# Another order of the steps in the steady batches of a three-stage mixer kernel

## The chip, the cores and the metric

The kernel runs on one core of a Trainium2 chip. The metric is the time of one execution on the device in microseconds (us), the median of several runs. The chip's engines work in parallel, each through its own list of instructions in order: TensorE (PE, with its weight loads shown as PEld), VectorE (DVE), ScalarE (ACT), GpSimd (POOL) and SyncE (SP), which here only issues DMAs. Where an instruction needs the result of another engine, or a buffer that another engine still reads, it waits on a semaphore, and all that stands behind it on its engine waits too.

## The reference

Three blocks follow each other for 8 batches of 576 rows. What matters here is the first two:

```python
q_s = softmax(q, axis=-1)            # each head's row of 64, with +1e-9 in the divisor
k_s = softmax(k, axis=2)             # over the sequence
kv = np.einsum('bhsd,bhse->bhde', k_s, v)
x = np.einsum('bhsd,bhde->bhse', q_s, kv)     # then heads side by side: 576 x 512

h = np.maximum(x @ w_in, 0.0)        # 576 x 1024
u, v = h[..., :512], h[..., 512:]
v_n = (v - mean(v)) / np.sqrt(var(v) + 1e-06)
v_s = np.einsum('ts,bsd->btd', w_spatial, v_n) + b_spatial[None, :, None]
y = (u * v_s) @ w_out
```

The third block takes y: theta = y @ w_theta, y·cos(theta) and y·sin(theta) mixed over the sequence with two 576 x 576 matrices, and a last product with w_ch. Its weights come as float64.

## The kernel before, in words

Every float32 product is made of three products of parts: each operand is split into a high part (rounded to the format that TensorE multiplies at full rate) and a low part (the rest), and hi·hi, hi·lo and lo·hi are summed in PSUM. So behind nearly every product stand a cast on ScalarE, which makes the high part, and a subtraction on VectorE or POOL, which makes the low part.

The kernel has two phases. In the first, a loop over the 8 batches runs the first two blocks and stores y; in the second, from about 600 us on, it runs the third block. The weights of the third block are converted from float64 (their bits are taken apart by integer steps on VectorE and ScalarE) during the first phase, a piece at a time, and stored to DRAM.

The order of the work in the first phase is written out by hand, as strings of words. `run` takes a string and emits, for each word, that step's instructions on all engines; there is no scheduler behind it. Batches 0 and 1 have strings of their own (`PLANS`), batch 7 too (`LAST`); batches 2 to 6 use `PLAN`. A number behind a word is the tile, or for words of q and k how many batches ahead; a `v` or `p` behind it puts the subtraction on VectorE or POOL. The words that matter:

- `V0`..`V4`: products of x with the v half of w_in for 128 rows (V4 for the last 64). `v`: ReLU on ScalarE (L488; for tile 4 L491 to L493), statistics on VectorE (L495 to L498), the power -1/2 on POOL (L499). `N`: normalisation on VectorE (L511), cast on ScalarE (L516; L519 and L520 for tile 4), subtraction on POOL (L517) or VectorE (L521).
- `U0`..`U3`: products with the u half; `r`: their ReLU on ScalarE (L535).
- `T0`..`T3`: transposes of the next batch's q on TensorE (L435, L438); `t`: their split (ScalarE L448, then L449). `X`: the product of that q with k·v, `x` its split. `S`: the spatial product of the normalised v; `G`: times u (VectorE L550), cast (ScalarE L551), subtraction (L552). `Y`: the last product, `y`: its copy (ScalarE L566) and store.
- q: `ldq` loads it, `qmax`, `qsub` (POOL L408), `qexp` (ScalarE L411), `qsum` (VectorE L422), `qmul` (POOL L430). k: `ldk`, `kmax` (VectorE L279 to L287), `kt`, `kr`, `kbc`, `kmb`, `ksub` (POOL), `kexp`; `K` the product of k and v (L353), `kn` its division (VectorE L368 to L385).
- `B`: the first half of a conversion (L219 to L244), after which the next pieces are loaded; `P`: its second half (L246 to L264), with two stores.

PSUM holds three buffers of two banks for V, K, U, T, X, S and Y (`big()`), so a product can only start when the buffer that was freed first has been read by whoever splits or rectifies it, and two buffers of one bank for the transposes of k's maximum. V0 of a batch needs the x of that batch, which the batch before made.

Of the kernel before, what the change touches and what calls it, by code (L numbers as in the profile page):

```python
# [30 lines left out]
ORDER = "u1 u0 u2 v3 u3 v2 v1 v0 s0 s3 s5 s2 s4 s1 o0 o2 o1 o3"  # L31
LOADS = "ldk1 ldq1 ldv1 ldw2 ldw4"
PLAN = (
# [3 lines left out]
)  # L37
PLANS = {
# [934 lines left out]
```

## Time and profile before

| | |
|---|---|
| median of 3 runs | 1045.49 us (1042.97 to 1045.59) |
| the profiled execution | 1045.59 us, of which the span of the trace is 1043.8 us |
| PE busy | 990.2 us, 95% of the span |
| PEld busy | 936.0 us, 90% |
| DVE, ACT, POOL busy | 636.5 us (61%), 417.3 us (40%), 385.6 us (37%) |
| V0 of batches 2, 3, 4 starts at | about 199, 265.8, 333.9 us |

A busy share is the part of the span in which an engine worked on an instruction. TensorE's is high, so the few microseconds in which it waits, and the engine that it then waits for, are what the order of the other engines' work can change. "Granted clock" is the share of TensorE's full clock (2.4 GHz) that it was given. In the rows of a timeline the first number is the start in us from the span's start, the second the duration in us, and brackets give the idle time of the engine just before and the engine, tile and line that ended it.

### The profile page before, as it was taken

How to read it: one execution, taken by the hardware profiler on the slowest of the kernel's cores; microseconds unless marked ns; L12 is line 12 of the kernel's file. 1: busy time of each engine (PE TensorE's matmuls, PEld its weight loads, DVE VectorE, ACT ScalarE, POOL GpSimd, SP SyncE). 2: the span in 40 equal slices, each digit the busy share in tenths (PEclk: the TensorE clock that was granted, in tenths of full speed). 3: DMA queues.
4: the chain of work that ended last, by engine and by line, in shares of the span. 5: the costliest groups of instructions: out<-in, count | busy, mean ns of one | idle time of the engine just before them, and what ended most of it. 6: DMA issues, size and time to landing. Idle time of an engine off the chain costs nothing.

```text
span 1043.8 us, 16301 instructions
## 1 busy us (share of the span) xinstructions
PE 990.2 (95%) x6688; PEld 936.0 (90%) x6688; DVE 636.5 (61%) x985; ACT 417.3 (40%) x671; POOL 385.6 (37%) x349
## 2 busy tenths in 40 slices
PE   4687999999999999999999999999999999999998
PEld 3567899999889899899999999999999999989998
DVE  7787868776676666766524745457363927374622
ACT  3545546543454444534524533234231515152410
POOL 6266147454545525545313323222132313121220
PEclk9888999999999999999999999999999999999999
DMA  7541441342414323431042336111111002010011
GB/s 262 192 126 41 175 163 43 133 158 85 178 68 159 120 92 113 158 110 44 21 167 81 126 125 136 46 46 47 56 46 47 37 10 90 13 57 35 2 46 46
DMA packets 37370, 96.50 MB, mean 92 GB/s; under 512 B 7088, under 2 KB 15792, under 8 KB 33200
## 3 DMA queue, kind: packets, MB, share of 16 engines
q1 hardware_dynamic: 33744, 85.96, 22.8%
q0 software_dynamic: 3552, 9.50, 3.2%
q8 instruction: 52, 0.85, 0.3%
q14 instruction: 22, 0.18, 0.1%
HBM read 67.08 MB, written 28.38 MB: 91 GB/s over the span
## 4 chain that ended last, share of the span: by engine, by line
PE 65%; DVE 10%; ACT 3%; issue 2%; DMA 1%; SPq 0%; ACTq 0%
PE ps L164 47%; PE pb L172 10%; PE ps L172 5%; DVE t L511 1%; PE pb L657 1%; DVE sm L495 1%; DMA st<-in_w_tok 1%; DVE q_s L422 1%; DVE t L282 1%; ACT u L535 1%; DVE kvl L385 1%; ACT vn L516 1%; DVE t L287 1%; PE ps L353 0%; DVE qt L449 0%
## 5 line engine op out<-in xcount | busy, mean ns | idle before, releaser
L164 PE MATMUL ps<-sp,vn 128*128 128x288 f32 x1472 | 211.7, 300 | 7.3 <-ACT vn L516 2.7
L164 PEld LDWEIGHTS ps<-sp,vn 128*128 128x128 f32 x1472 | 202.8, 192 | 9.9 <-ACT vn L516 2.9
L164 PE MATMUL ps<-g,wo 128*128 128x288 f32 x1104 | 160.6, 297 | 0.8 <-DVE wo L261 0.3
L164 PEld LDWEIGHTS ps<-g,wo 128*128 128x128 f32 x1104 | 151.0, 189 | 2.0 <-ACT t L566 0.7
L730 POOL TENSOR_TENSOR qt<-u,uh 128x576 fp32r<-128x576 f32 x31 | 44.2, 1426 | 217.7 <-ACT uh L728 217.7
L728 ACT CAST uh<-u 128x576 fp32r<-128x576 f32 x32 | 21.6, 674 | 216.1 <-DVE u L725 216.1
L164 PE MATMUL ps<-xh,w 128*128 128x288 f32 x512 | 93.4, 302 | 8.1 <-ACT w L257 8.1
L172 PE MATMUL ps<-w,xh 128*128 128x512 f32 x320 | 97.9, 398 | 3.3 <-ACT t L488 2.8
L164 PE MATMUL ps<-uh,w 128*128 128x288 f32 x496 | 91.8, 299 | 0.0
L164 PEld LDWEIGHTS ps<-xh,w 128*128 128x128 f32 x512 | 78.6, 194 | 9.1 <-ACT w L257 8.3
L172 PE MATMUL pb<-w,xh 128*128 128x512 f32 x256 | 81.3, 398 | 0.0
L552 POOL TENSOR_TENSOR g<-t,g 128x576 fp32r<-128x576 f32 x24 | 35.3, 1471 | 111.7 <-ACT g L551 111.7
L172 PEld LDWEIGHTS ps<-w,xh 128*128 128x128 f32 x320 | 59.2, 189 | 17.0 <-ACT t L488 3.5
L164 PEld LDWEIGHTS ps<-uh,w 128*128 128x128 f32 x496 | 73.6, 188 | 0.3
L499 POOL TENSOR_TENSOR mv<-mv,neg_half 128x1 f32<-128x1 f32 (+1 forms) x40 | 28.2, 709 | 91.7 <-DVE mv L498 91.6
L495 DVE BATCH_NORM_STATS2 sm<-t 128x6 f32<-128x512 f32 (+1 forms) x40 | 27.3, 682 | 52.3 <-ACT t L488 46.7
L725 DVE TENSOR_TENSOR u<-ps,kb 128x576 f32<-128x576 f32 x16 | 12.1, 758 | 73.6 <-PE ps L164 73.6
L164 PE MATMUL ps<-xl,w 128*128 128x288 f32 x256 | 56.0, 301 | 0.0
L172 PEld LDWEIGHTS pb<-w,xh 128*128 128x128 f32 x256 | 47.0, 188 | 9.8
L551 ACT CAST g<-t 128x576 fp32r<-128x576 f32 x32 | 21.6, 674 | 84.9 <-DVE t L550 84.8
L164 PE MATMUL ps<-sp,wo 128*128 128x288 f32 x336 | 53.9, 296 | 0.0
L164 PE MATMUL ps<-qt,w 128*128 128x288 f32 x248 | 53.0, 295 | 0.0
(208 smaller groups left out, 2029.2 us busy)
## 6 DMA issues: line engine op xcount, KB each, us to landing
vb<-in_v SPq DMA_DIRECT2D x8, 1300.0 KB, 6.3
y<-t SPq DMA_DIRECT2D x32, 288.0 KB, 2.3
out<-t SPq DMA_DIRECT2D x31, 288.0 KB, 2.1
qb<-in_q SPq DMA_DIRECT2D x7, 1152.0 KB, 5.2
kb<-in_k SPq DMA_DIRECT2D x6, 1152.0 KB, 7.8
st<-in_w_tok SPq DMA_DIRECT2D x9, 576.0 KB, 4.8
tok_d<-st SPq DMA_DIRECT2D x18, 288.0 KB, 2.2
qb<-y SPq DMA_DIRECT2D x4, 1152.0 KB, 5.2
```

Of the source, the lines that this page charges most:

```text
L164: nc.tensor.matmul(out=ps[:, c, 0:CH], lhsT=a, rhs=w[:, c * CH:(c + 1) * CH], start=first and i == 0, stop=final and i == last,)
L172: nc.tensor.matmul(out=ps, lhsT=a, rhs=w, start=(i == 0), stop=(i == last))
L282: nc.vector.tensor_tensor(out=m[p0:p0 + 64, c0:c0 + 256], in0=m[p0:p0 + 64, c0:c0 + 256], in1=kb[p0:p0 + 64, 2048:2304], op=ALU.max,)
L287: nc.vector.tensor_tensor(out=m, in0=m, in1=kb[:, c:c + 512], op=ALU.max)
L385: nc.vector.tensor_tensor(out=kl[p0:p0 + 64, :, :, e0:e0 + 64], in0=kn[p0:p0 + 64], in1=f(kh[p0:p0 + 64, :, :, e0:e0 + 64]), op=ALU.subtract,)
L495: nc.vector.bn_stats(out=bs[0:n], in_=vr[0:n])
L499: nc.gpsimd.tensor_tensor(out=mv[0:n, 1:2], in0=mv[0:n, 1:2], in1=neg_half[0:n, 0:1], op=ALU.pow)
L551: nc.scalar.copy(out=g_s[m], in_=g)
L552: eng.tensor_tensor(out=g_s[4 + m], in0=g, in1=f(g_s[m]), op=ALU.subtract)
L725: nc.vector.tensor_tensor(out=halves(u_s[m]), in0=ps[:, :, 0:CH], in1=halves(y1[b % 2][:, m, :]), op=ALU.add)
L728: nc.scalar.copy(out=st["uh"][:, m, :], in_=u_s[m])
L730: eng.tensor_tensor(out=qt_s[m], in0=u_s[m], in1=f(st["uh"][:, m, :]), op=ALU.subtract)
```

## The change

`PLAN`, the table of the steady batches, stands in another order; nothing else is touched. The first line of it before and after:

```diff
@@ -31,10 +31,10 @@
 PLAN = (
-    "qexp1 V0 V1 v0 v1 qsum1 V2 v2 qmul1 K1 ldv2 kn1 N0 V3 v3 ldk2 V4 v4 U0 N1 N2 U1 r0 B0p U2 N3 "
...
+        "V0 v0 N0 V1 qexp1 qsum1 qmul1 v1 V2 v2 K1 kn1 V3 V4 v3 v4 U2 N3 N4v N1 U0 ldk2 r0 N2 B0p ldv2 "
...
```

The words are the same, with these exceptions: one `B` has become `B0s` (that conversion's sign is taken on ScalarE and multiplied on, instead of set by a step on VectorE), and `G1` has become `G1v` (its subtraction on VectorE instead of POOL). What moves: v0's steps and N0 stand ahead of q's exponential, N3 and N4 ahead of N1 and N2, the u products come in the order 2 0 3 1, k's maximum stands ahead of S1 and G1, X1 behind S2, X2 behind Y0, the load of q behind S3, q's maximum and subtraction behind x product 2 and k's subtraction, and the last two conversions' second halves at the end.

On ScalarE at the start of a steady batch (q's exponential is L411, the ReLUs of v tiles L488, the cast of v tile 0 `vn_80`), before:

```order
L411 ACTIVATE qb<-qb 128x2304
L488 ACTIVATE t_3201<-ps 128x512
L488 ACTIVATE t_3209<-ps 128x512
L488 ACTIVATE t_3233<-ps 128x512
L384 CAST kvh<-kn 64x4x64 x2
L516 CAST vn_80<-t_3201 128x512
```

and after:

```order
L488 ACTIVATE t_3187<-ps 128x512
L516 CAST vn_80<-t_3187 128x512
L411 ACTIVATE qb<-qb 128x2304
L488 ACTIVATE t_3220<-ps 128x512
L488 ACTIVATE t_3241<-ps 128x512
L384 CAST kvh<-kn 64x4x64 x2
```

The ReLU and the cast of tile 0 moved ahead of the exponential, the other two ReLUs stayed behind it.

On ScalarE beside the u products (L535 are their ReLUs, `vn_81` to `vn_83` the casts of v tiles 1 to 3, `vn_88` and `vn_89` those of tile 4, L223 to L236 the first conversion's steps), before:

```order
L516 CAST vn_81<-t_2538 128x512
L516 CAST vn_82<-t_2562 128x512
L535 ACTIVATE u<-ps 128x576
L223 ACTIVATE t_2710<-t_2710,rebase 128x576
L235 ACTIVATE t_2712<-st 128x576
L236 ACTIVATE t_2711<-t_2711 128x576
L516 CAST vn_83<-t_2624 128x512
L519 CAST vn_88<-t_2642 64x512
L520 CAST vn_89<-t_2642 64x512
L535 ACTIVATE u<-ps 128x576
```

and after:

```order
L516 CAST vn_83<-t_2632 128x512
L519 CAST vn_88<-t_2640 64x512
L520 CAST vn_89<-t_2640 64x512
L516 CAST vn_81<-t_2549 128x512
L535 ACTIVATE u<-ps 128x576
L516 CAST vn_82<-t_2570 128x512
L223 ACTIVATE t_2716<-t_2716,rebase 128x576
L235 ACTIVATE t_2718<-st 128x576
L236 ACTIVATE t_2717<-t_2717 128x576
L535 ACTIVATE u<-ps 128x576
```

The casts of tiles 3 and 4 moved from between the first two ReLUs to ahead of the first, the cast of tile 2 to behind it; the conversion's three steps stay between the two ReLUs.

On VectorE beside the spatial products (`t_2891` and `t_2858` hold k's maximum, L550 are the gates' products with u, `qt_94` the low half of t2), before:

```order
L550 TENSOR_TENSOR t_2887<-ps,u 128x576
L279 TENSOR_TENSOR t_2891<-kb 128x512
L282 TENSOR_TENSOR t_2891<-t_2891,kb 64x256 x2
L287 TENSOR_TENSOR t_2891<-t_2891,kb 128x512 x2
L449 TENSOR_TENSOR qt_94<-ps,qt_93 128x576
```

and after:

```order
L279 TENSOR_TENSOR t_2858<-kb 128x512
L282 TENSOR_TENSOR t_2858<-t_2858,kb 64x256 x2
L287 TENSOR_TENSOR t_2858<-t_2858,kb 128x512 x2
L550 TENSOR_TENSOR t_2893<-ps,u 128x576
L552 TENSOR_TENSOR g<-t_2893,g 128x576
L449 TENSOR_TENSOR qt_94<-ps,qt_93 128x576
```

The product of gate 1 moved from ahead of k's maximum to behind it, and its subtraction, on POOL before, stands here too.

## Rows read from the trace of the kernel before

**Rows 1.** Waits of the weight loads, 190 to 542 us: us in total, times, longest

```profile
PEld ps L435 <- POOL vn L517: 7.3, 5, 1.8
PEld ps L164 <- DVE qt L449: 4.0, 7, 0.8
PEld ps L164 <- ACT u L535: 2.7, 5, 0.6
```

**Rows 2.** Timeline of TensorE in batch 3: V0, U0, last of U3, T0, S0, X0, X2

```profile
265.77 0.63 PE L172 MATMUL ps<-w,xh 128*128 128x512 f32 x2
...
283.65 0.43 PE L164 MATMUL ps<-xh,w 128*128 128x288 f32 x2
...
296.18 0.43 PE L164 MATMUL ps<-xh,w 128*128 128x288 f32 x2
298.17 0.63 PE L435 MATMUL ps<-turned,qb 128*128 128x128 f32 x4 [1.56 <-POOL vn L517]
...
299.23 3.99 PE L164 MATMUL ps<-sp,vn 128*128 128x288 f32 x28 [0.32 <-ACT u L535]
...
303.88 0.80 PE L164 MATMUL ps<-qt,kvh 128*128 128x288 f32 x4
...
314.28 0.79 PE L164 MATMUL ps<-qt,kvh 128*128 128x288 f32 x4 [0.56 <-DVE qt L449]
```

**Rows 3.** Timelines of ScalarE, VectorE and POOL in batch 3, V0 to T0

```profile
271.73 2.13 ACT L411 ACTIVATE qb<-qb 128x2304 f32<-128x2304 f32 x1 [4.09 <-POOL qb L408]
...
286.00 0.58 ACT L491 COPY t<-ps 64x512 f32<-64x512 f32 x1
...
291.79 0.77 ACT L223 ACTIVATE t<-t,rebase 128x576 int32<-128x576 int32 x1
...
297.43 0.64 ACT L535 ACTIVATE u<-ps 128x576 f32<-128x576 f32 x1
...
274.38 0.69 DVE L495 BATCH_NORM_STATS2 sm<-t 128x6 f32<-128x512 f32 x1 [6.16 <-ACT t L488]
...
280.45 0.32 DVE L368 TENSOR_SCALAR sm<-ps 64x4 f32<-64x4 f32 x2
...
281.92 1.71 DVE L385 TENSOR_TENSOR kvl<-kn,kvh 64x256 fp32r<-64x256 f32 x2
...
289.51 0.99 DVE L511 TENSOR_SCALAR t<-t,mv 128x512 f32<-128x512 f32 x2
...
292.59 1.67 DVE L241 SCALAR_TENSOR_TENSOR t<-st,t 128x576 int32<-128x576 int32 x1 [1.35 <-ACT t L223]
294.18 2.10 DVE L511 TENSOR_SCALAR t<-t,mv 128x512 f32<-128x512 f32 x2
297.56 0.82 DVE L521 TENSOR_TENSOR vn<-t,vn 64x512 fp32r<-64x512 f32 x1 [1.27 <-ACT vn L520]
...
293.82 1.73 POOL L237 TENSOR_TENSOR t<-t,t 128x576 f32<-128x576 f32 x1 [0.18 <-ACT t L236]
```

**Rows 4.** Batch 4: T0 and S0 (timeline); a stretch's busy times, then PEclk, DMA share, GB/s

```profile
366.31 0.63 PE L435 MATMUL ps<-turned,qb 128*128 128x128 f32 x4 [1.56 <-POOL vn L517]
...
367.37 5.48 PE L164 MATMUL ps<-sp,vn 128*128 128x288 f32 x28 [0.32 <-ACT u L535]
...
368.00:370.00 2.00, 2.00 (x10) 2.00 (x10) 1.97 (x4) 1.35 (x2) 0.00 (x0) 0.50 0.85 278
```

**Rows 5.** By line: ns min/median/max, first and last start; then batch 3's timeline

```profile
L511 DVE TENSOR_SCALAR t<-t,mv x39: 529/539/1653, 77.1 to 558.1; 128x512 f32<-128x512 f32 x31, 64x512 f32<-64x512 f32 x8
L282 DVE TENSOR_TENSOR t<-t,kb x16: 416/420/1568, 5.2 to 447.7; 64x256 f32<-64x256 f32 x16
...
310.11 2.00 DVE L282 TENSOR_TENSOR t<-t,kb 64x256 f32<-64x256 f32 x2
310.26 1.57 POOL L552 TENSOR_TENSOR g<-t,g 128x576 fp32r<-128x576 f32 x1 [3.55 <-ACT g L551]
```

**Rows 6.** DMA issues, 312 to 326 us: line, queue, count, KB each, us to landing

```profile
qb<-in_q SPq DMA_DIRECT2D x1, 1152.0 KB, 5.0
```

More of the change, by code (lines that the diff above doesn't have):

```diff
@@ L33 @@
 PLAN = (
[3 rows of a table removed]
-)
[3 rows of a table added]
+    )
 PLANS = {
```

4 rows, old and new, of the table PLAN are left out of this document.

## The prediction

> **What bounds the kernel now.** I read the busy shares first: TensorE is the busy engine almost everywhere, so what the change can give is the time in which TensorE waits inside the five batches that use the changed table (batches 2 to 6, from about 199 to 537 us of the span), and what it can cost is a new wait there. Next I read TensorE's waits in that stretch, on the weight loads, since the busy time of the matmuls includes a modelled tail that hides the small gaps [rows 1]. Three releasers stand there: 7.3 us before the first product of q's transposes (T0, once in each of the five batches), 2.7 us before the first spatial product (S0, once in each), 4.0 us before products of x that wait for a low half of q (X0 and X2). Together 14.0 us, 2.8 a batch. Then I read one batch, the one whose V0 starts at 265.77, to see the places [rows 2]: the last u product's last pair starts at 296.18 and T0 only at 298.17, S0 at 299.23 after another wait, X0 at 303.88, X2 at 314.28 after 0.56 idle.
>
> Why T0 is late is in the rows of the other engines [rows 3]. T0 writes into the PSUM buffer of the second u product, and that is freed by r1, the ReLU at 297.43 on ScalarE, which ended when T0 began. (The view of rows 1 names POOL's subtraction, which ended just before r1.) S0 needs the buffer of the third product, freed by the next ReLU. r1 was ready long before, but ScalarE works in order: ahead of it stand the casts of v tiles 3 and 4, and these wait for VectorE's normalisation at 294.18, which stands behind the conversion's step on VectorE (L241), which waits for ScalarE's first conversion step at 291.79. All of that is late because v0's ReLU stands behind q's exponential, which starts only at 271.73, 6.0 us after V0, when POOL has finished subtracting q's maximum.
>
> **The change part by part**, in times after a batch's V0 (for the batch of rows 2, U0 is at +17.9 and one u product lasts 3.2 us, so T0 could run at +30.7 and S0 at +31.1).
>
> *q's subtraction earlier, v0 and its normalisation ahead of q's exponential.* q's maximum now stands behind x product 2 instead of behind the last conversion, so POOL goes from k's subtraction straight to q's. I put POOL's end at about +2, where it was at +5.9 (q's exponential waited 4.09 us for it [rows 3]). ScalarE then does v0's ReLU at +3.1, VectorE its statistics (0.69 for L495, about 0.4 for the two small ones) and the normalisation (0.54 alone [rows 5]), ScalarE the cast by about +6.6, then q's exponential (2.13) to +8.7. Before, that exponential ended at +8.1. VectorE from there to kn (the division of k·v) took 6.6 us before (273.86 to 280.45 [rows 3]) with three v statistics in it; now two stand there, so about 5.5, and kn begins at +14.2 at the latest instead of at +14.7. v0's statistics and normalisation cost nothing: VectorE is idle there.
>
> *N3 and N4 ahead of N1, N2 and ahead of the conversion.* kn's 3.2 us (280.45 to the end of L385 at 283.63 [rows 3]) end at +17.3, v3's statistics at +18.3. v3's ReLU no longer waits for v0's cast. V4 ends at +17.9; its copy, addition, ReLU and statistics took 3.6 us before (286.00 to the normalisation at 289.51 [rows 3]) with 0.5 of queueing, so N3's normalisation starts at about +21.2. N3, POOL's power, N4, three casts and the subtraction L521: 4.2 us before (294.18 to 298.38), of which 1.1 is the slow pair of normalisations (2.10 against 0.99 for the pair at 289.51 [rows 3]); alone, with the power between, 3.6. So N1 starts at about +24.8. N1, its cast and r0 take 1.7: r0 ends at +26.5, and U1, which needs that buffer, starts at +27.5 (1.0 spare). N2's cast, the three ScalarE steps of the conversion (0.77 for the first [rows 3], about 2.0 for the three) and r2 end at +29.5: T0 at +30.7 has 1.1 spare. The next cast and r3 end at +30.7: S0 at +31.1 has 0.4 spare. Both waits go. What is late next is X0: POOL's addition for the conversion (1.73 at 293.82 [rows 3]) ends at +30.6, VectorE's six conversion steps and ScalarE's two follow, and t0's low half is ready at +35.4, with T1 finished at +35.4. I leave 0.1 to 0.2 a batch for X0 and 0.2 once for S0 in batch 2, whose exponential starts later, 1.2 us in all.
>
> *U products 2 0 3 1.* The same 96 matmuls. It only changes which ReLU frees whose buffer, as used above; zero.
>
> *k's maximum earlier, G1's low half on VectorE.* k's maximum now stands ahead of G1 on VectorE instead of behind it. Before, its second line (L282) ran beside POOL's subtraction for G1 and took 2.00 for the two where one alone takes 0.42 [rows 5]; X2 waited for what stood behind it. Now G1 has no POOL part, and G0's POOL part ends about 0.7 us before k's maximum starts. So k's maximum lasts 1.15 us less, G1's product ends about 7.3 us after X0's start, G1's low half and t2's low half about 9.5 after, and T3, which needs the latter's buffer, has its turn 10.0 after. X2 moves behind Y0, where its operands are long ready. So the 0.7 us of X2 go as well. If the two lines take 2.00 again, T3 waits 0.65 and S3 0.25: about the loss that X2 had before. I take the free value, since the only POOL step near it ends before, and keep the other for the range.
>
> *The q load behind S3, q's maximum behind X2.* The load of q takes 5.0 us [rows 6]; it is issued when T3 has read the old q, at about +46, so it lands at +51, and VectorE reaches q's maximum at about +52. Hidden. The loads of k and v change places, both are issued at +13 when k·v is done and needed some 25 and 60 us later: zero.
>
> *Conversions later.* Two of three now end in the Y products' shadow; VectorE has some 2 us left before v0's statistics. y1's copy last on ScalarE: its buffer is taken by V2, 5.6 us into the next batch, and the copy ends at +1.5. Zero.
>
> **The sum.** 14.0 us of waits go, 1.2 stay: 12.8. A second term: in the profiled execution S0 of batch 4 took 5.48 us instead of 3.99, because the granted clock fell to 0.50 (1.2 of 2.4 GHz) from 368 to 370 us, just after T0's wait of 1.56 us [rows 4]. Two other batches had the same wait and no fall, so the fall is not certain, but its cause among these rows is the pause, and the pause goes: 1.5 us. 1045.59 for the profiled execution (equal to the median of the runs, 1045.49) − 12.8 − 1.5 = 1031.3; I say 1031.5.
>
> **The rivals.** *1. VectorE and POOL collide in the new places.* N4's normalisation and POOL's subtraction for N3 become ready within 0.3 us of each other. The pair at 294.18 shows the price, 1.1 us [rows 3]; L511 reaches 1.65 us at worst [rows 5]. With 1.1 more, r3 ends 0.7 after S0 could start and X0 loses 0.5: 1.0 us more a batch, 5 in all, 1036.5. If k's maximum collides instead, 0.9 in four batches, 1035. For it: every v tile passes this place. Against: the power releases VectorE first.
> The Trainium skill (SBUF — State Buffer, section "SBUF: two separate sides") says the ports that VectorE and GpSimd share are an exclusive lock, held for the whole instruction by whichever starts first. By that rule, N4 would lose nothing if first and 1.3 us, a whole POOL subtraction, if second; the sum would be 1031.5 or about 1037. The trace agrees with an all-or-nothing price: L282's pair ended 0.28 us after POOL's subtraction [rows 5].
> *2. The chain only slides.* r2 now stands behind three conversion steps and two casts. If my chain is off by 2 to 3 us (a stage or temporary buffer not free in time), T0 and S0 wait as before: 1038 to 1047.
> *3. Slower: q's load becomes late.* On VectorE q's maximum stands ahead of the low half of x2, and Y2 needs the buffer which that frees. With the load landing at +51, Y2 at about +58 has 2.5 us spare. From a load of 7.5 us on, each further microsecond stops TensorE in four batches; to eat 14 us it must take 11 us, and at 12 it gives 1050. Against it: 5.0 us in the row, and no other large transfer near that place.
>
> **How the numbers follow.** Forecast, 1029.5 to 1034: 0.60. Rival 1, 1034 to 1037.5: 0.22. Rival 2: 0.08 faster than 1042, 0.05 within 0.3%. Rival 3 or another new wait, slower: 0.05. So faster by over 0.3% (3.1 us, about what a measurement of this kernel can tell from no change) 0.90, within 0.05, slower 0.05. The range takes the first two cases, 1029.5 to 1037.5, a little over 0.8.
>
> **What the profile after would show.** TensorE's weight loads wait no longer before T0 and under 0.3 us before S0; the distance from V0 to V0 is 64.5 to 65 us instead of 68.1; q's exponential starts near +6.6 with v0's ReLU ahead of it; L282 takes 0.42 each; X0 is the largest remaining wait. Wrong would be: a wait of TensorE on L488 or L566 at V0 to V3, T3 waiting for t2's low half, N4's L511 at 1.2 us or more, or Y2 waiting behind q's maximum.

## Result and profile after

| | before | changed |
|---|---|---|
| median | 1044.23 us (1040.88 to 1045.59, 4 runs) | 1027.03 us (1025.81 to 1030.26, 4 runs) |
| ratio | | 0.9845, 95% interval 0.981 to 0.988 |
| span of the profiled execution | 1043.8 us | 1024.4 us |
| start of the span to V0 of batch 0 | 59.97 us | 55.97 us |
| V0 of batch 0 to V0 of batch 2 | 138.98 us | 139.11 us |
| V0 of batch 2 to V0 of batch 7 | 337.59 us | 321.87 us |
| V0 of batch 7 to the end | 507.3 us | 507.4 us |

The lower half of the table shows where the time went: the starts of the V0 products in TensorE's timeline cut the span into four parts. The batches that the change touches gave 15.7 us. 4.0 us more came before batch 0's first product, where the two kernels have the same instructions. The change made the kernel 1.5% faster; the forecast, 1029.5 to 1037.5 us, was too slow.

The waits of TensorE's weight loads from 190 to 542 us (us in total, times, longest), first of the changed kernel, where they answer to [rows 1], then two rows of the kernel before that stood under those of [rows 1] in the same answer:

```profile
PEld ps L172 <- DVE xl L449: 0.9, 1, 0.9
PEld ps L164 <- DVE qt L449: 0.7, 3, 0.3
```

```profile
PEld ps L353 <- issue: 1.5, 3, 0.5
PEld ps L172 <- DVE xl L449: 0.5, 1, 0.5
```

Neither T0 nor S0 waits any more. What is left is 1.6 us, of which 0.5 was there before; the 0.9 is one V product at the start of batch 2, and in the second trace of the changed kernel (e2, below) it is 0.5. A third wait went that the forecast didn't book: 1.5 us before the K products (L353).

TensorE's timeline of batch 3 in the changed kernel: V0, first and last pair of the u products, T0, S0, X0. It answers to [rows 2]:

```profile
260.43 0.63 PE L172 MATMUL ps<-w,xh 128*128 128x512 f32 x2
...
277.95 0.43 PE L164 MATMUL ps<-xh,w 128*128 128x288 f32 x2
...
290.49 0.42 PE L164 MATMUL ps<-xh,w 128*128 128x288 f32 x2
...
290.75 0.60 PE L435 MATMUL ps<-turned,qb 128*128 128x128 f32 x4
...
291.21 3.96 PE L164 MATMUL ps<-sp,vn 128*128 128x288 f32 x28
...
295.67 0.79 PE L164 MATMUL ps<-qt,kvh 128*128 128x288 f32 x4
```

No row has a wait in brackets. The u products begin at +17.5 (before +17.9), T0 comes at +30.3 (+32.4), S0 at +30.8 (+33.5).

The other engines in the same batch (first ScalarE: v0's ReLU, its cast, q's exponential, v3's ReLU, the second and third ReLU of u; then VectorE: v0's normalisation, kn, v3's statistics, N3, N4, N1 with N2, k's maximum; then POOL's subtraction for N3), which answer to [rows 3]:

```profile
263.43 0.60 ACT L488 ACTIVATE t<-ps 128x512 f32<-128x512 f32 x1
266.56 0.62 ACT L516 CAST vn<-t 128x512 fp32r<-128x512 f32 x1 [2.54 <-DVE t L511]
267.09 2.13 ACT L411 ACTIVATE qb<-qb 128x2304 f32<-128x2304 f32 x1
...
276.29 0.60 ACT L488 ACTIVATE t<-ps 128x512 f32<-128x512 f32 x1
...
288.81 0.64 ACT L535 ACTIVATE u<-ps 128x576 f32<-128x576 f32 x1
...
290.02 0.65 ACT L535 ACTIVATE u<-ps 128x576 f32<-128x576 f32 x1
...
265.99 0.55 DVE L511 TENSOR_SCALAR t<-t,mv 128x512 f32<-128x512 f32 x1 [0.67 <-POOL mv L499]
...
274.31 0.32 DVE L368 TENSOR_SCALAR sm<-ps 64x4 f32<-64x4 f32 x2
...
277.70 0.69 DVE L495 BATCH_NORM_STATS2 sm<-t 128x6 f32<-128x512 f32 x1
...
281.21 0.53 DVE L511 TENSOR_SCALAR t<-t,mv 128x512 f32<-128x512 f32 x1
282.18 0.54 DVE L511 TENSOR_SCALAR t<-t,mv 64x512 f32<-64x512 f32 x1 [0.45 <-POOL mv L499]
...
284.65 1.00 DVE L511 TENSOR_SCALAR t<-t,mv 128x512 f32<-128x512 f32 x2
...
299.85 0.85 DVE L282 TENSOR_TENSOR t<-t,kb 64x256 f32<-64x256 f32 x2
...
282.47 1.40 POOL L517 TENSOR_TENSOR vn<-t,vn 128x512 fp32r<-128x512 f32 x1 [0.32 <-ACT vn L516]
```

L282's pair takes 0.85 us (2.00 in [rows 5]), no normalisation is stretched (2.10 for a pair in [rows 3]), and the two ReLUs of u on which T0 and S0 hang in the forecast's working end at +29.0 and +30.2, ahead of T0's and S0's turn; before, T0's began at +31.7.

### The profile page after: what moved, and what is told of

The parts are those of the page before. It is cut to its first block, busy times and chain, and to the rows that moved or that the text cites. A ratio compares the mean times of both kernels' runs of the same rounds, so it can differ in the third digit from the quotient of the medians.

```text
span 1024.4 us, 16271 instructions
## 1 busy us (share of the span) xinstructions
PE 979.7 (96%) x6688; PEld 930.0 (91%) x6688; DVE 648.7 (63%) x990; ACT 420.2 (41%) x671; POOL 381.3 (37%) x344
## 4 chain that ended last, share of the span: by engine, by line
PE 84%; DVE 8%; POOL 3%; ACT 3%; issue 2%; DMA 0%; POOLq 0%; ACTq 0%; DVEq 0%
PE ps L164 61%; PE pb L172 10%; PE ps L172 8%; PE ps L353 2%; PE pb L657 1%; PE ps L435 1%; POOL qb L408 1%; DVE t L287 1%; POOL sp L197 1%; DVE t L229 1%; DVE q_s L422 0%; DVE t L241 0%; DVE t L282 0%; DVE t L225 0%; ACT qb L411 0%
## 5 line engine op out<-in xcount | busy, mean ns | idle before, releaser
L552 POOL TENSOR_TENSOR g<-t,g 128x576 fp32r<-128x576 f32 x19 | 27.9, 1469 | 104.1 <-ACT g L551 72.4
L725 DVE TENSOR_TENSOR u<-ps,qb 128x576 f32<-128x576 f32 x16 | 12.1, 758 | 63.4 <-PE ps L164 63.4
L172 PE MATMUL ps<-w,xl 128*128 128x512 f32 x128 | 50.5, 394 | 0.5 <-DVE xl L449 0.5
```

The lines of the kernel that those rows point to most:

```text
L172: nc.tensor.matmul(out=ps, lhsT=a, rhs=w, start=(i == 0), stop=(i == last))
L552: eng.tensor_tensor(out=g_s[4 + m], in0=g, in1=f(g_s[m]), op=ALU.subtract)
L725: nc.vector.tensor_tensor(out=halves(u_s[m]), in0=ps[:, :, 0:CH], in1=halves(y1[b % 2][:, m, :]), op=ALU.add)
```

## The experiments

Each run has a label (e1 to e12, s1 to s6), and most of the texts below, written before the run, name a theory and a rival with the time that each would give. All are compared by one length in their traces, from V0 of batch 2 to V0 of batch 7 (**the stretch**), since the start-up differs from run to run by more than most edits do. T0 and S0 are of batch 3, after its V0; "q ends" is the end of POOL's subtraction of q's maximum. The stretch of s6 contains a clock fall of about 1.3 us (its batch 5 took 67.99 us where its batch 4 took 66.89, and in the undisturbed traces batch 5 is some 0.2 shorter than batch 4).

| kernel | stretch | q ends | T0 | S0 |
|---|---|---|---|---|
| before, without the clock fall (e1) | 336.6 | +5.9 | +32.4 | +33.5 |
| v0 first alone (s3) | 327.2 | +5.9 | +30.4 | +31.4 |
| early q alone (s1) | 330.8 | +2.2 | +30.8 | +31.9 |
| k's maximum first alone (s2) | 338.7 | +5.9 | +32.4 | +33.5 |
| the same, S2 ahead of X1 (s4) | 337.1 | +5.9 | +32.4 | +33.5 |
| the same, X2 behind Y0 too (s6) | 333.0 | +5.5 | +32.0 | +33.0 |
| new first half, old second half (e3) | 327.5 | +5.9 | +30.4 | +31.2 |
| old first half, new second half (e4) | 327.3 | +3.2 | +30.7 | +31.8 |
| changed (after, e2) | 321.9, 321.4 | +3.3 | +30.3 | +30.8 |
| changed, q later (e11) | 327.8 | +6.8 | +31.2 | +32.1 |
| changed, q latest (e5) | 332.8 | +8.1 | +32.5 | +33.3 |

**Both kernels once more**, unchanged, one execution each.

> The kernel before, once more, for its trace. Theory A (the time before the first batch varies from run to run with the pace that TensorE is granted at the start, and has nothing to do with the order): V0 of batch 0 starts anywhere from 56 to 60 us, where the first trace has 59.97. From V0 of batch 2 to V0 of batch 7 it takes 336 to 338 us again (337.6 in the first trace); without a fall of the clock beside T0 it is 336. Rival (the start is a property of the kernel): V0 of batch 0 at 59.9 to 60.1 again.

> The changed kernel, once more, for its trace. Theory A: V0 of batch 0 starts anywhere from 56 to 60 us (55.97 in its first trace); from V0 of batch 2 to V0 of batch 7 it takes 321.5 to 322.3 us (321.9 in the first trace). Rival (the start belongs to the kernel): V0 of batch 0 at 55.9 to 56.1 again.

The kernel before took 1040.73 us with V0 of batch 0 at 56.06 and a stretch of 336.56; the changed one 1026.63, 56.71 and 321.38. So the 4.0 us are the start-up's and not the change's, and the clock fall of [rows 4] is not in every execution: batch 4 took 68.13 us here and 69.23 in the first trace. Free of both, the change is worth 15.2 us. In 20 traces V0 of batch 0 stood between 55.7 and 60.1, in five of them at 59.69 or more. Most of it comes from the very first K products: in the six traces with V0 at 58.8 or later the first 40 took about 11.1 us, in the others 7.8 to 9.3 (TensorE's timeline, 40 products in one row; the first row of the kernel before, the second of the changed one):

```profile
17.04 11.11 PE L353 MATMUL pb<-vb,kb 128*128 128x130 f32 x40 [6.29 <-ACT kb L340]
```

```profile
16.82 8.29 PE L353 MATMUL pb<-vb,kb 128*128 128x130 f32 x40 [6.30 <-ACT kb L340]
```

**Halves of the order.** The table up to T0 as changed and from T0 on as before, and the other way round.

```diff
 e3
-"qexp1 V0 V1 v0 v1 qsum1 V2 ... r2 B r3 "
+"V0 v0 N0 V1 qexp1 qsum1 qmul1 ... r3 r1 B "
 "T0 t0 S0 G0 T1 X0 S1 t1 x0 G1 kmax2 ... Y2 kexp2 Y3 y2 P0v y3"
 e4
 "qexp1 V0 V1 v0 v1 qsum1 V2 ... r2 B r3 "
-"T0 t0 S0 G0 T1 X0 S1 t1 x0 G1 kmax2 ... Y2 kexp2 Y3 y2 P0v y3"
+"T0 t0 S0 G0 T1 X0 x0 t1 kmax2 S1 G1v ... Y3 y3 qsub2 y1"
```

> The changed order up to the steps ahead of T0 (v tiles, k times v, u products), and the order of before from T0 on. Theory: the waits ahead of T0 go (7.3 us over the five batches), the fall of the clock with them (1.5), the pause ahead of k times v (1.5). X2 still waits (2.8). q's subtraction is late as before, ends at +5.9 on POOL and holds the power of v0, so the chain to r3 comes 1 us later than in the changed kernel: S0 waits about 0.5 and X0 0.7 in a batch. From V0 of batch 2 to V0 of batch 7: 326 to 329 us. Rival (the first part needs no early q): 324.7, that is the changed kernel and X2's 2.8.

> The order of before up to the steps ahead of T0, and the changed order from T0 on. Theory: X2's waits go (2.8 us over the stretch); T0 and S0 still wait, though q's exponential, which stands first, comes 4 us earlier, at +2, so that v0's ReLU is 4 us earlier and T0 waits about 0.5 instead of 1.7, as in batch 2 of the first trace. From V0 of batch 2 to V0 of batch 7: 328 to 332 us. Rival (T0's wait hangs on the order of the normalisations alone, not on when q's exponential ends): T0 waits 1.7 again, 334 to 335.

e3: 1031.99 us (1031.74 to 1034.69), ratio 0.9907 (0.9883 to 0.9931), stretch 327.5, as its theory had it. e4: 1033.02 us (1032.62 to 1035.8), ratio 0.992 (0.9891 to 0.9948), stretch 327.3, 0.7 below its theory's range. Each half alone gives 9, both together 15: 3 us are claimed by both. In e4 T0 came at +30.7 although the first half was the old one. So the second half does part of what the first half does; s1 below shows that it does so by its early q.

**The order of the normalisations** (N1 and N2 ahead of N3 and N4 again) **and of the u products.**

```diff
 e9
-"U2 N3 N4v N1 U0 ldk2 r0 N2 B0p ldv2 U3 U1 r2"
+"U2 N1 N2 U0 ldk2 r0 B0p ldv2 N3 N4v U3 U1 r2"
 e8
-"U2 N3 N4v N1 U0 ldk2 r0 N2 B0p ldv2 U3 U1 r2 P0v r3 r1 B"
+"U0 N3 N4v N1 U1 ldk2 r0 N2 B0p ldv2 U2 U3 r1 P0v r2 r3 B"
```

> The changed order, but the normalisations of v tiles 1 and 2 ahead of those of 3 and 4 again, with the first ReLU and the first conversion between the two pairs, as before. Theory: the ReLU that frees T0's buffer stands behind the casts of tiles 3 and 4 and the conversion again; T0 waits 1 to 1.5 us and S0 0.5 to 1 in a batch, X0 as before: 330 to 334 us from V0 of batch 2 to V0 of batch 7. Rival (with q's exponential and v0 early this order would do as well): 321 to 323.

> The changed kernel with the u products in the order 0 1 2 3 again. The prediction put their order at nothing: 320.7 to 322.2 us from V0 of batch 2 to V0 of batch 7, as the changed kernel's 321.4 and 321.9. Rival: the order is what lets the ReLU that T0 waits for come early, and T0 waits 0.5 us or more in each batch: 324 us or more.

e9: stretch 321.15, T0 at +30.3: its rival held. e8: 321.42, its theory held. Neither order is worth anything here. The first contradicts the prediction's account of T0.

**One edit at a time, from the kernel before.**

```diff
 s1
-"ksub2 Y0 Y1 y0 X3 x3 y1 B qmax2 qsub2 Y2"
+"ksub2 Y0 Y1 y0 qmax2 qsub2 X3 x3 y1 B Y2"
 s2
-"G1 kmax2 T2"
+"kmax2 G1v T2"
 s3
-"qexp1 V0 V1 v0 v1 qsum1 V2 v2 qmul1 K1 ldv2 kn1 N0 V3"
+"V0 v0 N0 V1 qexp1 qsum1 qmul1 v1 V2 v2 K1 ldv2 kn1 V3"
```

> The kernel before with one edit: v0 and its normalisation stand ahead of q's exponential; q's subtraction and all else as before. Theory: q's exponential starts at +7.6 instead of +6.0 (it queues behind the cast of the normalised tile), but the normalisation is gone from the queue ahead of the u products' ReLUs, so the ReLU that T0 waits for starts some 1.2 us earlier and T0 comes at +31.2: 329 to 333 us against 336.6. Rival: the later exponential costs what the place saves: 335 to 338 us, and T0 stays at +32.4.

s3: 1035.63 us, stretch 327.24, 9.3 us less, better than the theory's 329 to 333. T0 waits no more, although q's subtraction is as late as before and q's exponential 1.6 us later. The timeline of batch 3 in this kernel (V0 at 265.02): on ScalarE q's exponential, v3's ReLU and the ReLU of u for which T0 waits; on VectorE kn, v3's statistics, N1 with N2, N3 with N4:

```profile
272.60 2.12 ACT L411 ACTIVATE qb<-qb 128x2304 f32<-128x2304 f32 x1
...
281.72 0.60 ACT L488 ACTIVATE t<-ps 128x512 f32<-128x512 f32 x1
...
294.64 0.64 ACT L535 ACTIVATE u<-ps 128x576 f32<-128x576 f32 x1
...
279.82 0.32 DVE L368 TENSOR_SCALAR sm<-ps 64x4 f32<-64x4 f32 x2
...
283.20 0.69 DVE L495 BATCH_NORM_STATS2 sm<-t 128x6 f32<-128x512 f32 x1
...
286.71 0.99 DVE L511 TENSOR_SCALAR t<-t,mv 128x512 f32<-128x512 f32 x2
...
291.38 2.10 DVE L511 TENSOR_SCALAR t<-t,mv 128x512 f32<-128x512 f32 x2
```

and the same place in the kernel before (V0 at 265.77): on VectorE v0's normalisation and v3's statistics, on ScalarE v0's cast and v3's ReLU:

```profile
283.67 1.15 DVE L511 TENSOR_SCALAR t<-t,mv 128x512 f32<-128x512 f32 x1
286.00 0.69 DVE L495 BATCH_NORM_STATS2 sm<-t 128x6 f32<-128x512 f32 x1 [1.19 <-ACT t L488]
...
284.85 0.62 ACT L516 CAST vn<-t 128x512 fp32r<-128x512 f32 x1 [2.53 <-DVE t L511]
285.38 0.59 ACT L488 ACTIVATE t<-ps 128x512 f32<-128x512 f32 x1
```

kn stands at +14.8 with the edit and at +14.7 without. The gain is behind it: before, v0's normalisation followed kn on VectorE, its cast waited for it on ScalarE, and v3's ReLU, whose data was there, waited behind that cast. With v0 done ahead, v3's statistics come at +18.2 instead of +20.2, and everything up to T0's ReLU moves by the same 2.05 us; 1.4 us of the 9.3 are the K products, which start 0.28 earlier in each batch. The slow pair of normalisations is still there (2.10 at 291.38), and T0 does not mind.

> The kernel before with one edit: q's maximum and subtraction of the next batch stand behind k's subtraction, ahead of the third block's last projection, instead of ahead of the third y tile. Measured is the stretch from the first V product of batch 2 to that of batch 7 (336.6 us before without the clock fall, 321.4 changed). Theory Q: the early subtraction moves the whole chain of the head, so the first turn T0 comes at +30.7 after V0 instead of +32.4, as it did with the old head and the new tail; nothing else moves: 327 to 330 us. Rival N: the chain only slides, the normalisations' order holds T0 back as before: 335 to 337 us.

s1: 1038.55 us with a start-up of 59.69, stretch 330.78: 5.8 us less, 1.6 in each of batches 3 to 5. T0 came where theory Q put it (+30.8); the stretch is 0.8 above its range, and the rival is out. T0 still waits (2.6 us in five). Early q and v0 first alone give 5.8 and 9.3, but largely the same microseconds: both take the 1.5 us before the K products, and s3 leaves nothing of T0's 7.4 us for s1's 4.8, while both leave the waits for q's low half as they were (4.4 and 4.7). No run has just these two edits together.

> The kernel before with one edit: k's maximum stands ahead of the second gate and that gate's low half on VectorE, as in the changed kernel. Theory K: the pair of L282 takes 0.85 us instead of 2.00, the waits of X2's weight load for the q tile (4.0 us in seven) go, and nothing else: 332 to 333.5 us from V0 of batch 2 to V0 of batch 7 against 336.6. Rival: with the old chain of q the gain is slack and is handed back as a longer wait of T0: 335.5 to 337 us.

s2: 1043.79 us, stretch 338.70: 2.1 us more, outside both expectations. The longest new wait of the weight loads in that kernel; TensorE's row for the third spatial product (S2) of batch 3; VectorE's k maximum (three rows) and the second gate's product just ahead of it:

```profile
PEld ps L164 <- DVE t L550: 5.3, 4, 1.3
```

```profile
308.77 4.00 PE L164 MATMUL ps<-sp,vn 128*128 128x288 f32 x28 [1.10 <-DVE t L550]
```

```profile
305.02 0.69 DVE L279 TENSOR_TENSOR t<-kb 128x512 f32<-128x512 f32 x1
305.74 0.85 DVE L282 TENSOR_TENSOR t<-t,kb 64x256 f32<-64x256 f32 x2
306.63 1.42 DVE L287 TENSOR_TENSOR t<-t,kb 128x512 f32<-128x512 f32 x2
307.96 0.75 DVE L550 TENSOR_TENSOR t<-ps,u 128x576 f32<-128x576 f32 x1
```

k's maximum is fast, as wanted, but it now stands ahead of G1's product, which frees the PSUM buffer that S2 needs next in the old order.

**What the second half's gain is made of.**

```diff
 s4
-"t1 x0 G1 kmax2 T2 t2 X1 x1 S2 G2 X2"
+"t1 x0 kmax2 G1v T2 t2 S2 G2 X1 x1 X2"
 s5
-"T2 t2 X1 x1 S2 G2 X2"
+"T2 t2 S2 G2 X1 x1 X2"
 s6
-"G1 kmax2 T2 t2 X1 x1 S2 G2 X2 x2 T3 ldq2 kt2 t3p kr2 S3 ... Y0 Y1 y0 X3"
+"kmax2 G1v T2 t2 S2 G2 X1 x1 kt2 T3 S3 ldq2 t3p kr2 ... Y0 X2 y0 x2 Y1 X3"
```

> The kernel before with two edits: k's maximum ahead of the second gate with that gate's low half on VectorE (which alone gave 338.7 us from V0 of batch 2 to V0 of batch 7 against 336.6), and the third spatial product with its gate ahead of the second product of x. Theory: the wait of 1.1 us before the third spatial product goes, since that product no longer needs the buffer that the second gate frees, and so does the wait before the third product of x: 333 to 334.5 us. Rival: the wait moves to the next user of that buffer: 336 to 339 us.

> The kernel before with one edit: the third spatial product with its gate ahead of the second product of x; k's maximum stays behind the second gate. Theory: the third product of x comes at the same place and still waits some 0.6 us a batch for the q tile whose low half stands behind k's maximum: 336 to 337.5 us from V0 of batch 2 to V0 of batch 7 against 336.6. Rival: the order on TensorE is what matters and k's maximum nothing: 333 to 334.5 us, as with both edits.

> The kernel before with the changed kernel's second half on TensorE and k's maximum: k's maximum ahead of the second gate, the third spatial product ahead of the second x product, k's transposes ahead of T3, the third x product behind Y0; head of the batch, q's maximum and subtraction as before. Theory: the three moves of the second half belong together; with the third x product behind Y0 nothing is handed on to the fourth spatial product any more (3.8 us in the run without that move), so the 0.6 to 0.8 us a batch of the q tile's wait go and T0 stays at +32.4: 332.5 to 334 us from V0 of batch 2 to V0 of batch 7 against 336.6. Rival: the second half gains only through q's early subtraction: 336 to 338 us.

s4: stretch 337.13, the rival held. s5: 342.66 (about 1.3 of it a clock fall), worse than both expectations. s6: 332.99, in the theory's range with a clock fall of about 1.3 in it and some 0.8 below it without; T0 came 0.4 earlier than the theory had it, with q's subtraction ending at +5.5. Of the waits of the weight loads, the one that is new in s4, and then the three longest of s6:

```profile
PEld ps L164 <- DVE xl L449: 3.8, 5, 1.1
```

```profile
PEld ps L435 <- POOL vn L517: 6.8, 5, 1.7
PEld ps L164 <- ACT u L535: 2.7, 5, 0.6
PEld ps L164 <- DVE qt L449: 1.1, 3, 0.4
...
```

In s4 S2 waits no more, but X1 and X2 stand together ahead of T3, and S3 waits for the buffer that x1's low half frees. With X2 behind Y0, s6 has neither, and what is left is T0's and S0's wait of the first half. The three moves (with k's transposes ahead of T3 and q's load behind S3, which moved with them) give 3.6 us (4.9 without the fall), where k's maximum alone, the exchange of S2 and X1 alone and the two together gave nothing or lost. X2 behind Y0 was not tried alone. Not all of the 4.9 is the freed buffers': of the waits, 3.3 us for q's low half went (4.4 in e1, 1.1 here), but also the K products' 1.5 and 0.6 before T0, which come with q's end at +5.5. Where q is early anyway, the second half gives 3.5 us (e4 against s1).

**The place of k's maximum in the changed kernel**: behind the second gate, the gate's low half on POOL (e6) or on VectorE (e7).

```diff
-"kmax2 S1 G1v T2"
+"S1 G1 kmax2 T2"    (e6)
+"S1 G1v kmax2 T2"   (e7)
```

> The changed order, but gate 1 ahead of k's maximum again with its subtraction on POOL, as before. Theory: POOL's subtraction runs beside k's maximum again, its two lines L282 take 2.0 us together instead of 0.85, and t2's low half and gate 2 stand behind it: T3 and S3 wait 0.7 to 1.0 us together in four batches. 324.5 to 326 us from V0 of batch 2 to V0 of batch 7. Rival (the place of k's maximum costs nothing): 321 to 322.5.

> The changed order, but gate 1 ahead of k's maximum, its subtraction still on VectorE. POOL has nothing beside k's maximum. Theory: L282 takes 0.85 us for the two, but k's maximum starts only after gate 1, 2 us later than in the changed kernel, so T3 and S3 wait 0.7 to 1.0 us together in four batches all the same: 324 to 326 us from V0 of batch 2 to V0 of batch 7. Rival (the collision with POOL was all that X2's wait came from): 321 to 322.5.

Stretches 323.46 (between its theory and its rival) and 324.81 (its theory held). L282 by line in e6 and in e7 (ns min/median/max, first and last start):

```profile
L282 DVE TENSOR_TENSOR t<-t,kb x8: 416/988/1567, 240.8 to 435.9; 64x256 f32<-64x256 f32 x8
```

```profile
L282 DVE TENSOR_TENSOR t<-t,kb x8: 416/420/423, 238.7 to 434.9; 64x256 f32<-64x256 f32 x8
```

e7 has no collision and is still the slower one: k's transposes wait for its later maximum (1.9 us in four, on L287). So with POOL beside it the collision is there, but it is not what the place costs: the later place without any collision loses 3.4 us against e2's 321.4, and with the gate's low half given to POOL, collision and all, it loses 2.1.

**How late q may be.** In the changed kernel, q's maximum and subtraction back towards the end of the table.

```diff
-"kmb2 X2 qmax2 x2 X3 Y1 x3 B0s P0v ksub2 P0v Y2 y2 kexp2 Y3 y3 qsub2 y1"
+"kmb2 X2 x2 X3 Y1 x3 B0s P0v ksub2 P0v qmax2 qsub2 Y2 y2 kexp2 Y3 y3 y1"   (e5)
+"kmb2 X2 x2 X3 Y1 x3 B0s P0v ksub2 qmax2 qsub2 P0v Y2 y2 kexp2 Y3 y3 y1"   (e11)
```

> The changed order, but q's maximum and subtraction behind the conversions again, as before (ahead of Y2 instead of behind X2). Theory: POOL ends q's subtraction near +6 of the next batch instead of +2, v0's power and normalisation, q's exponential and all that follows come about 1 us later; T0's ReLU still has room, S0 waits about 0.5 and X0 0.7 in a batch. From V0 of batch 2 to V0 of batch 7: 324.5 to 326.5 us (321.4 to 321.9 for the changed kernel). Rival (the place of q's maximum does not matter, the normalisations alone do): 321 to 322.5.

> The changed kernel with q's maximum and subtraction placed between the two places tried so far, so that POOL ends the subtraction near +6 after V0, as in the kernel before (+3.3 in the changed kernel: 321.4 to 321.9 us; +8.1: 332.8 us). Theory: with v0 and its normalisation ahead of q's exponential there is slack up to about +6, so the early q is worth nothing by itself: 321 to 323 us. Rival: the loss grows evenly from +3.3 on, 0.47 us a batch for each microsecond: 327 to 329 us.

e5: stretch 332.77, far above what was expected. A batch of it whose V0 starts at 330.61: POOL's subtraction, the power of v0's statistics behind it, v0's normalisation, its cast and q's exponential:

```profile
334.04 4.63 POOL L408 TENSOR_TENSOR qb<-qb,q_m 128x512 f32<-128x512 f32 x5 [6.73 <-DVE q_m L402]
338.63 0.55 POOL L499 TENSOR_TENSOR mv<-mv,neg_half 128x1 f32<-128x1 f32 x1
...
339.21 0.55 DVE L511 TENSOR_SCALAR t<-t,mv 128x512 f32<-128x512 f32 x1 [3.88 <-POOL mv L499]
...
339.79 0.62 ACT L516 CAST vn<-t 128x512 fp32r<-128x512 f32 x1 [5.59 <-DVE t L511]
340.32 2.12 ACT L411 ACTIVATE qb<-qb 128x2304 f32<-128x2304 f32 x1
```

Here v0 first turns against the kernel: its power waits on POOL behind q's subtraction, and q's exponential waits on ScalarE behind v0's cast, so a late q pays twice. e11 landed at +6.8 instead of the intended +6, with 327.81. The two expectations can be told apart by T0: +30.3 for q ending at +3.3, +30.4 at +5.9 (e3, s3), +31.2 at +6.8, +32.5 at +8.1. That is flat up to about +5.9 and then one for one (1.24 us for 1.24 us between the last two). So T0 has the slack, and e11 lay beyond it; the stretch itself, 327.81, is what the rival gave. S0 has less: in e3, whose first half is the changed kernel's, it comes at +31.2 instead of +30.8. The second ReLU of u stands there at +29.3, 0.94 later than in the changed kernel (e3's row, V0 at 261.18):

```profile
290.50 0.64 ACT L535 ACTIVATE u<-ps 128x576 f32<-128x576 f32 x1
```

v0's power waits there on POOL until q's subtraction ends. So behind the v0 edit the early q is still worth something, at S0.

**Batch 1 and the join to batch 2.** Batch 1 has a table of its own. e10 gives it the steady order; e12 only moves its last step, k's exponential.

```diff
 e10, table of batch 1
-"V0 v0 kexp1 N0v V1 v1 V2 K1 qexp1 V3 kn1 v2 ... X3 x3 kexp2"
+"V0 v0 kexp1 N0 V1 qexp1 qsum1 qmul1 v1 V2 ... Y3 y3 qsub2 y1"
 e12, table of batch 1
-"qsub2 y2 Y3 y3 X3 x3 kexp2"
+"qsub2 y2 kexp2 Y3 y3 X3 x3"
```

> The changed kernel with batch 1, which has a table of its own, given the order of the steady batches too, k's exponential behind the statistics of v0. Theory: batch 1 had the same wait of T0 for the late normalisations, so its distance from V0 to V0 falls from 66.2 us to 64.5 to 65.5, that of batch 2 from 64.9 to 64.5, the rest stays at 321 to 322 us from batch 2 to batch 7: 1.0 to 2.0 us less than the changed kernel at the same start-up. Rival: k's exponential delays q's in batch 1, T0 waits, 66 us or more, no gain.

> The changed kernel with k's exponential at the end of batch 1's own table put ahead of its last y tile, as the steady batches have it. Theory: v0's ReLU of batch 2, which stands behind that exponential at +4.4, comes at +3.0, and batch 2 takes 64.3 us from V0 to V0 as it did behind a batch 1 with the steady order, against 64.9 to 65.4: 320.6 to 321.0 us from batch 2 to batch 7, total 0.5 to 1 us below the changed kernel at the same start-up. Rival: the exponential waits for k's subtraction and holds the copies of the last y tiles, so batch 2 begins later: 321.5 us or more, or batch 1 longer than 66.2 us.

e10: 1027.68 us (1026.85 to 1028.65), ratio 0.9867 (0.9847 to 0.9887): batch 1 took 68.0 us from V0 to V0 instead of 66.2, batch 2 64.2 instead of 65.4 (64.9 in e2). Batch 1 loses more than the join gains: the rival held. e12: 1031.37 us (1030.43 to 1031.86), ratio 0.9897 (0.9875 to 0.9919), slower than the changed kernel; the rival held. Its row at the join, in the first V product of batch 2, and the two microseconds behind it (length, TensorE's busy time, granted clock, DMA share, GB/s):

```profile
201.85 1.22 PE L172 MATMUL ps<-w,xh 128*128 128x512 f32 x2 [2.97 <-ACT xh L448]
```

```profile
202.00:204.00 2.00, 2.00 (x5) 0.50 0.39 147
```

The exponential waits on ScalarE for k's subtraction, and a cast of x behind it, which V0 needs, waits along. Batch 2 took 69.0 us, 4.1 more than in e2: the wait of 2.97, and the clock, which fell to 0.50 behind it. No version was clearly faster than the changed kernel.

## Why the prediction was wrong

**The anchor and one missing term failed; the rest of the sum held, though not for all of its reasons.** The sum was 1045.59 − 12.8 − 1.5.

- *Anchor.* 1045.59 was taken as the kernel's time because it equals the median of the three runs shown. It contained a start-up of 60.0 us. The later runs of the kernel before had medians of 1042.5, 1042.6 and 1042.1 (seven runs each; two single ones 1045.7 and 1045.4), and the changed kernel's trace has a start-up of 56.0. This term was too high by 4.0 us between the two traces and by some 3.3 against those medians, and is most of the miss: from 1042.3 the same sum gives 1028.0, 1.0 above the 1027.03 measured.
- *Waits that go.* 14.0 us were booked. The 1.5 before the K products was not, and this is the step that failed inside the batches: the view calls its releaser "issue", and the prediction took the three rows that name an engine. In the five traces with v0's ReLU at +8.0 (before, e1, s2, s4, s5) the K products of batch 3 start at +8.68, right behind that ReLU; where the ReLU starts at +7.6 or earlier, at +8.4. So it was the same late ReLU of v0, 0.28 us a batch, 1.4 in five.
- *Residual.* 1.2 booked, 1.1 found (1.6 less the 0.5 that was there before).
- *Clock.* 1.5 booked for batch 4; the distance from V0 to V0 lost 1.1 (69.23 against 68.13). The fall came in 3 of the 18 batches 3 to 5 of the six traces with T0's long wait (before, e1, s2, s4, s5, s6), each time just behind that wait, and in these batches in no trace without it. The one other fall between 150 and 545 us is e12's, behind its wait of 2.97 us. That the pause is the cause is not shown beyond this: 15 such waits had no fall. The row of s6: length, TensorE's busy time (x count), granted clock (0.5 is 1.2 of 2.4 GHz), DMA share, GB/s:

```profile
432.00:434.00 2.00, 2.00 (x11) 0.54 0.71 250
```

With these: 14.0 + 1.5 − 1.1 + 1.1 = 15.5 of the 15.7 us measured.

**The steps, one by one.**

- *q's exponential and v0.* Times right: exponential at +6.7 (forecast +6.6), kn at +13.9 (+14.2 at the latest); POOL ended at +3.3, not +2. But the step named both edits as one need. s3 shows that v0 first takes T0's wait alone, and e3 that the early q adds only 0.1 us to T0 then; s1 shows that the early q without v0 first gets most of T0 too. In the changed kernel a late q is no longer harmless, though: e5 loses 11 us.
- *N3 and N4 ahead of N1, N2 and the conversion.* Every time of the chain was 0.4 to 0.6 us early or right (N3 +20.8 for +21.2, N1 +24.2 for +24.8, third ReLU's end +30.2 for +30.7); 0.2 of it is a slip, since the prediction's own terms put N3 at +21.0. The reason was wrong: this order was given T0's and S0's waits, and e9 takes it away at no cost. What did the work is a half sentence of that step: v3's ReLU no longer waits for v0's cast.
- *U products 2 0 3 1.* Zero, as forecast (e8).
- *k's maximum.* L282's 0.85 and X2's vanished wait are as forecast. The credit was misplaced: the edit alone loses 2.1 us (s2). It needs S2 ahead of X1, which the prediction didn't mention, and X2 behind Y0, which it took for a side matter; together they give 3.6 to 4.9 us (s6), some 2 of it by q's earlier end.
- *q's load and its maximum behind X2.* Hidden: the load took 5.1 us, and Y2 doesn't wait. Rival 3 did not come.
- *Conversions later, y1 last, k's and v's loads exchanged.* Booked at zero; no new wait shows, and they were not tried alone.
- *Rival 1, collisions.* Did not come: N4 started at 282.18 and took 0.54, POOL's subtraction started at 282.47 inside it and took 1.40 against 1.29 for v0's. The Trainium skill (SBUF — State Buffer, section "SBUF: two separate sides") says that, where VectorE's instruction uses the shared pair of ports too, whichever of the two starts first holds it for the whole instruction. The trace agrees in direction only: the one that came second was longer, but by 0.11 us, with 0.25 us of N4 still to run.
- *Rival 2, the chain only slides.* Did not come in the changed kernel, whose chain ran ahead of the forecast. With q late, in e5, it slid: T0 came 2.2 us later, 332.8 us.

**What stays open.** S0's wait (2.7 us in five batches before) does not go by one edit: it is 2.7 us in s1, 1.7 in s3 and 1.1 in e3; the last 1.1 went where q was early as well. And after s3's 9.3 and the second half's 3.5, some 2.4 us of the 15.2 have no edit of their own. The early q is the likely one: e3, which lacks it, waits 1.1 us for S0 and 1.0 more than e1 for q's low half. No run adds it alone. The start-up's own cause stays open too.

## What to carry to other kernels

When a step waits on an in-order engine, look for what stands ahead of it there and could have been done earlier in an idle stretch: moving one normalisation and its cast out of the queue gave 9.3 of 15.2 us, while the order of what stayed in that queue gave nothing. A move that frees one buffer sooner often delays another, so moves that share PSUM buffers are to be judged as a set: one of three alone lost 2.1 us, all three won 3.6 or more. And a step that is pulled ahead brings its own waits along: with v0 first, a late q cost the changed kernel 11 of its 15 us (e5). Compare parts of the span, not totals, and take the anchor from the median of many runs after looking at how its start-up differs.

## What the runs showed of the hardware

The first 40 K products took 11.11 us in one execution and 8.29 in another (278 and 207 ns each; 4.63 us, 116 ns each, in the steady batches), and with what follows the start-up differed by up to 4.4 us in 20 traces. The column of the granted clock has 1.00 in both, from 23 to 25 us, in which 10 matmuls ran before and 14 after (first the kernel before):

```profile
23.00:25.00 2.00, 2.00 (x10) 1.00 0.00 0
```

```profile
23.00:25.00 2.00, 2.00 (x14) 1.00 0.00 0
```

At which level the products ran there the rows don't tell. The Trainium skill (TensorE: Matmul & The Clock Gate, section "What's actually happening") says that how many matmuls run slow at a kernel's start changes from run to run, and that it is worth under 1% of the span. The size agrees: up to 4.4 of 1040 us, 0.4%, which here is more than the forecast's range left room for. That these products were slow for that reason no row here shows.
